# Six more key blocks with VectorE's exp, and a new written order, in an attention and gated-FFN kernel

## The chip, the cores and the metric

The kernel runs on one core of a Trainium2 chip. The metric is the device time of one launch in microseconds (us). The engines are TensorE (PE; its weight loads are shown apart as PEld), VectorE (DVE), ScalarE (ACT), GpSimd (POOL) and SyncE (SP), which starts most of the DMAs.

## The reference

```python
S, D, H, Dh, F = 2048, 512, 32, 16, 1792             # one batch, bfloat16
xn = layernorm(x)                                     # no gain, no bias
q, k, v = split(xn @ wqkv)                            # 32 heads of 16
p = softmax(einsum("qd,kd->qk", q, k) * Dh ** -0.5)   # for every head
attn = (p @ v).reshape(S, D) @ wo
gate, up = xn @ W_gate, xn @ W_up                     # 512 -> 1792
ffn = ((gate * (gate > 0)) * up) @ W_down
out = x + attn + ffn
```

The scores are 32 heads x 2048 x 2048, 134 million numbers, and each goes through an exp.

## The kernel before

**Tiling.** The 2048 queries are cut into four chunks of 512 (`c4`), the 32 heads into four groups of eight (`gg`), and each group into two halves of four heads (`ee`). That gives 32 rows, numbered 0 to 31 in the order (c4, gg, ee). A row runs over 16 key blocks (`kt`) of 128 keys. One key block of one row is four heads x 128 keys x 512 queries of scores. The layernorm, the projections of q, k and v, the gated FFN ("glu") and the output rows are background work, which stands between the attention's matmuls.

**Two kinds of key block.** A key block is done in one of two ways.

- *ACT's way.* Two units, each with scores of two heads in two banks of PSUM, one ACT exp over 128 x 1024 (L1365, `ring<-ps`), and then, when both units are there, one "PV stream" (`pv_stream`, L1244): eight matmuls of 64 x 32 weights on 512 columns, which add p @ v, and the row sums, into a bank of PSUM. PSUM has two places for the scores of a unit (pool `sc`, two banks each), so the scores of unit u+2 wait for the exp of unit u.
- *VectorE's way.* `quad` (L1312) makes four score banks, one at a time, out of the pool `b` of four banks that the projections, the FFN, the output and the PV sums use as well. A DVE instruction (L1320, "d1") adds a bias to a bank's scores and writes them as 16-bit integers, whose bits read as bfloat16 are a rough exp. Two more versions of all four banks together are made by adding a constant to the integers (one for each of two shifts): each either by one DVE instruction over 2048 columns (L1339, "d2" and "d3") or by two instructions of POOL (L1335, "p3"). All three versions go through PV, so that their errors average out: three PV streams instead of one.

The table `QUAD_AT` has one line for each row and one character for each key block. A dot is ACT's way. A digit is VectorE's way, and its bits say which of the two added versions POOL makes: 0 none, 1 the first, 2 the second, 3 both. The kernel before has 153 digits.

**The PE's tiles.** Nearly all matmuls use a 64 x 32 part of the array: four side by side in one half of its rows make one operation ("half"), and an operation of the other half may run at the same time. Scores of a key block are 16 matmuls, one PV stream is 8.

**The order.** No scheduler runs in the kernel: all engines' queues are in one written order. `PLAN` is a packed list that says, for each of its `PLAN_OPS` steps, which operation comes next, and for each operation that opens a buffer, which place of its pool it gets. `Graph.run` (L324) unpacks it, appends each operation to its engine's queue, and makes an operation that takes over a place wait for the ones that used it before:

```python
o = ops[at] if at < n else self.blank(at)
for t in o.acq:
    if t.slot is not None:
        continue
    t.slot = next(places)
    c = t.pool.cur[t.slot]
    if c is not None:
        for u in c.w + c.r:
            if u.eng != o.eng or o.eng not in ("PE", "ACT"):
                o.deps[u] = True
```

Each engine runs its queue in order, and waits on semaphores for what it needs of the others. A p3 of POOL also waits for the last d2 or d3 that stands ahead of it in the order. The integers lie in four buffers (pool `raw`), their added versions in five (pool `pat`), and ACT's exps in a ring of 16.

All matmuls of scores, PV, background and output are issued by one helper, L250. The last row is normalised at the end by DVE, PE and ACT (L1151 to L1168).

Of the kernel before, what the change touches and what calls it, by code (L numbers as in the profile page):

```python
# [16 lines left out]
S = 2048  # L17
D = 512
H = 32
DH = 16  # L20
F = 1792
# [25 lines left out]
NQ = 2  # L47
# [30 lines left out]
    "2...3..3..2..3..",  # L78
# [6 lines left out]
    "2...3..3..0..3..",  # L85
    "3...3..3..2..3..",
# [5 lines left out]
    "2...3..3..2..3..",  # L92
    "2...3..3..0..3..",
    "2...3..3..2..3..",
    "2...3..3..0..3..",
    "2...3..3..2..3..",
    "2...3..3..0..3..",
    "2...3..3..2..3..",
# [23 lines left out]
PLAN_OPS = 8248  # L122
PLAN = (
    "c-m!K1z;3M7v67n?{Wzd96~7)9Euky#fn1{v}hoK;8KbdcXx*Z#UWUc1S{?yij?ARg%p<nA>8f!Z)SJzHvEN<&E4+Ilka`+dvmFxr2dbKFK%6lf2^OxpPcvTGN*FSxG*2!#(Uzg@iI@fAXj{^<+x8@"
    "%6)Si-}BZZIh1?Wi;8boZof|$L0|XHm3{A9SJrLzy}8dF<9#T;*NnG~=Zyz+<6X!r<1XE12mQnqv4Rfy92EJAaiv>UfZpcj3mo26tqZQ$U$U%#_ciYGN&bQHBUf~J#l2=5&xoHaJB&+R@m)eUmxgY6"
    "1Mf<TVy*7=RX$=o=v_jrEyKoj@vvM?guuAZe1Kaql;**5!dTnG<bKeNI7+LmDA0wmjtHuEL0$U9ZE&$8Qryc8bEQY-YT!n=#1=+S<f4Xo@?W{UVg>|8pbR&RMXi6VU8KqKRjx=k#ie36ubayl(KlZZ"
    "Hkp@Zm}T5xJ)_w0XF*%xKB#iV=avr+x@m*ulCD_6H(%v;1K@*@uf*hc-3Kr$F6MW|ECM5~#yipxX1ho6K#?I4w=!QwxG%ZBoN;c4Gq+cx`6k)JEI2SPpBQc_9_EqpWxi+|cG5G(8XkzOFxxIx2)WG;"
    "v#>-|tRzVEh^;*em;WkE095*CSm<HqH|`M|cr09qT?N{VqVkBF%{%E!F2OyVSrjJo#C@^#5)-#ki(ELx!R42&{H1*&2Hxz52r$buahFFFHO%CC#9Q)JX4)?UB?Bn-@h~$EIv~rA8_Cs;WrYXK$Nit2"
    "M!^`XNhfIu!$pr-LS8yEID~)F1h<%6rs(#5!hPxRm9Y^lkGYG%5gr*R0~OLCGBU+!z=V64=^WYo$tfJMfyPTKzOG}v;bF$wOvcRc*~FY;Bv>(tiF*u~8(XJvKX15AfN<jhZuJo_&2ULV6kSIO6u07Z"
    "n^5&Yev|jYSj=N$RJvkR9J6dQw^K}4WnknQ2KJbTo4lwq%O)-%r<f?UuuDHk&%DjiSK&Se(yeb+R>Tduswg~lX?yeb(aF4Nkg+hqF8uHqwZ!ZoHmb)Pd?OPS5BUuDmX8s2!)cF~_zloVDiYqnivk~q"  # L130
    "nY1CwOy{3m@(zy-tptie8y<@zOv?m=nS1CyhNEu=B`7eOk-4-{f*<_M5>EDG7OrJlj3<qH<B}A0Uq6ShIT>w0_7VdV7WXDQb<H4KFK}%NhI8+iw?X?D-P<nA;$d8|bq!xzx2@%?Juea2d0J6Ycihz4"
    "iKpttb}qMXVl_42%G{@Q45=jhvlSWL=1(da;oV)g$rSi7X|g-_={ghMqMLJ*p}1~7rOW*c)nvS?_#*193-N&Jm2bY<vBgpM1wl8Rg-!aJs>hOTHhssvVvX}uy4D`TRBeJ=Dnik}C}X4+x2a?83x)z8"
    "P7M7D-$pVbhF-Mp(9NeUoO!Rm(9_&TEIgIe=U=4H*8F8n=~jp=p$ePY^|cgh5n-d%d3{m#82#JSWxiUqOr$1lsdSSV4fZs9w5f$mrt#t2l1_2~v;V<-Ua~WEtC}S<>(DK_7H`2Y3_dto2=#_e`(*Vt"
# [121 lines left out]
class Graph:  # L255
# [1162 lines left out]
```

## Time and profile before

| | |
|---|---|
| time, median of 3 runs (lowest to highest) | 685.26 us (685.21 to 687.11) |
| span of the profiled execution, first to last instruction | 684.2 us |
| busy, PE / DVE / ACT / POOL | 675.6 / 598.5 / 666.8 / 499.8 us |
| exps on ACT | 718 |
| d1 on DVE, d2 and d3 on DVE, p3 on POOL | 612, 83, 446 |
| matmuls on PE | 22262 |

The profile is of one execution; its own time is its span and about a microsecond around it. Matmuls are pipelined and their ends are modelled, so a PE that is busy is not a PE at its peak. A group's busy time is the union of its instructions; the mean ns of one is longer than union over count where instructions overlap. Lines (L1365) are those of the kernel before.

### The profile page before, as it was taken

The numbers are of one execution on the slowest core, as the hardware profiler recorded it, in microseconds if no ns is written. First come the engines' busy times: TensorE is split into PE (matmuls) and PEld (weight loads), VectorE is DVE, ScalarE is ACT, GpSimd is POOL, SyncE is SP. The second block draws the span as 40 slices with busy tenths as digits, with TensorE's granted clock in tenths as the row PEclk, the third lists the DMA queues.
The fourth block names the chain that finished last, engine by engine and source line by source line (L and its number), as shares of the span: only waits on it lengthen the run. The fifth ranks groups of instructions, "written<-read, shape, count | busy, mean of one in ns | idle before, by whom it ended". The sixth has DMA issues, their size and how long they took to land.

```text
span 684.2 us, 45020 instructions
## 1 busy us (share of the span) xinstructions
PE 675.6 (99%) x22262; PEld 345.9 (51%) x19654; DVE 598.5 (87%) x1012; ACT 666.8 (97%) x730; POOL 499.8 (73%) x507
## 2 busy tenths in 40 slices
PE   8999999999999999999999999999999999999998
PEld 4455454545555554554444455554554455555543
DVE  9958899999989787999999788889998887988875
ACT  6999999999999999999999999999999999999994
POOL 3323768678688778887587886888878868787792
PEclk9999999999999999999999999999999999999999
DMA  7430220113122021212101022120202012131011
GB/s 216 57 75 12 58 77 27 33 55 91 56 65 66 5 77 34 69 41 63 35 23 31 10 78 63 38 69 5 56 27 61 25 53 62 44 86 42 22 36 54
DMA packets 55940, 35.86 MB, mean 52 GB/s; under 512 B 19336, under 2 KB 51784, under 8 KB 55752
## 3 DMA queue, kind: packets, MB, share of 16 engines
q1 hardware_dynamic: 55464, 32.71, 17.4%
q8 instruction: 164, 2.69, 1.6%
q10 hardware_dynamic: 288, 0.26, 0.1%
q14 instruction: 24, 0.20, 0.1%
HBM read 26.35 MB, written 2.35 MB: 42 GB/s over the span
## 4 chain that ended last, share of the span: by engine, by line
PE 75%; ACT 18%; DVE 5%; issue 1%; DMA 0%; POOL 0%; ACTq 0%
PE ps L250 75%; ACT ring L1365 18%; DVE stats L726 1%; DVE qd L1320 1%; DVE xn_sb L739 1%; DVE v_aug L876 0%; DMA x_sb<-in_A_x_dram 0%; DVE qT L952 0%; DVE mv L727 0%; ACT xn_sb L1164 0%; DVE qd L1339 0%; DVE xnT L780 0%; POOL rstd L721 0%; DVE xnT L1075 0%; DVE kT L869 0%
## 5 line engine op out<-in xcount | busy, mean ns | idle before, releaser
L1365 ACT ACTIVATE ring<-ps 128x1024 bf16<-128x1024 f32 x718 | 660.4, 1141 | 2.9 <-PE ps L250 2.5
L1335 POOL TENSOR_TENSOR qd<-qd,ints 128x512 int32<-128x512 int32 x446 | 450.5, 1041 | 143.8 <-DVE qd L1339 73.2
L250 PE MATMUL ps<-qT,kT 64*32 64x512 bf16 x8192 | 448.7, 374 | 1.3 <-DVE qd L1320 0.4
L1320 DVE TENSOR_SCALAR qd<-ps 128x512 int16<-128x512 f32 x612 | 396.7, 685 | 51.9 <-PE ps L250 49.0
L250 PE MATMUL ps<-qd,v_aug 64*32 64x512 bf16 x3672 | 263.0, 375 | 1.1 <-issue 0.9
L250 PE MATMUL ps<-ring,v_aug 64*32 64x512 bf16 x2872 | 236.5, 374 | 0.1
L1300 PEld LDWEIGHTS <-kT 64*32 64x32 bf16 x7584 | 151.1, 92 | 126.6 <-issue 32.6
L1272 PEld LDWEIGHTS <-v_aug 64*32 64x32 bf16 x4544 | 108.7, 91 | 75.6 <-issue 20.4
L250 PE MATMUL ps<-xnT,wgs 64*32 64x512 bf16 x1792 | 137.6, 374 | 0.0
L250 PE MATMUL ps<-xnT,wus 64*32 64x512 bf16 x1792 | 136.4, 374 | 0.0
L250 PE MATMUL ps<-Wd,hT 64*32 64x512 bf16 x768 | 59.0, 375 | 0.0
L810 PEld LDWEIGHTS <-wgs 64*32 64x32 bf16 x1792 | 43.1, 91 | 31.5 <-issue 7.4
L810 PEld LDWEIGHTS <-wus 64*32 64x32 bf16 x1792 | 43.2, 91 | 29.8 <-issue 7.6
L1339 DVE TENSOR_SCALAR qd<-qd 128x2048 int16<-128x2048 int16 x83 | 56.1, 690 | 2.3 <-PE ps L250 2.2
L810 PEld LDWEIGHTS <-hT 64*32 64x32 bf16 x1792 | 40.2, 92 | 28.2 <-issue 4.2
L250 PE MATMUL ps<-Wv,hT 64*32 64x512 bf16 x512 | 45.7, 375 | 0.0
L250 PE MATMUL ps<-Wk,hT 64*32 64x512 bf16 x512 | 42.8, 375 | 0.4 <-DVE qd L1320 0.3
L1020 DVE SCALAR_TENSOR_TENSOR hT<-ps,up_sb 128x512 bf16<-128x512 f32 x56 | 38.4, 685 | 4.6 <-PE ps L250 4.2
L1016 DVE COPY up_sb<-ps 128x512 f32<-128x512 f32 x56 | 38.4, 685 | 3.1 <-PE ps L250 2.5
L250 PE MATMUL ps<-Wo_p,x_sb 64*32 64x512 bf16 x480 | 40.2, 374 | 0.6 <-issue 0.5
L250 PE MATMUL ps<-xnT,Wq 64*32 64x512 bf16 x480 | 36.2, 375 | 0.0
L250 PE MATMUL ps<-xnT,Wk 64*32 64x512 bf16 x480 | 35.0, 374 | 0.3 <-DVE xnT L780 0.3
(70 smaller groups left out, 263.8 us busy)
## 6 DMA issues: line engine op xcount, KB each, us to landing
rb<-rec_scr SPq DMA_DIRECT2D x31, 256.0 KB
wus<-in_B_W_up_dram SPq DMA_DIRECT2D x38, 128.0 KB, 2.8
wgs<-in_B_W_gate_dram SPq DMA_DIRECT2D x38, 128.0 KB, 3.3
xr_sb<-in_A_x_dram SPq DMA_DIRECT2D x16, 128.0 KB, 2.6
qT<-qf SPq DMA_DIRECT2D x120, 16.0 KB, 2.6
out_dram<-xn_sb SPq DMA_DIRECT2D x14, 128.0 KB, 2.0
x_sb<-in_A_x_dram SPq DMA_DIRECT2D x8, 128.0 KB, 2.8
x_sb<-oT SPq DMA_DIRECT2D x60, 16.0 KB, 2.5
```

The lines of the kernel that those rows point to most:

```text
L250: return e.add_instruction(mybir.InstMatmult(name=e.bass.get_next_instruction_name(), engine=mybir.EngineType.PE, ins=[e.lower_ap(x), e.lo ...
L726: G.op("DVE", 580, lambda e, m=m: e.bn_stats(stats[:, m, :], xs(m)), reads=[t_xm[m]], writes=[t_st], prio=pr, order=last_xn if m == 4 else ())
L739: G.op("DVE", 320, lambda e, m=m, t=t_n: e.tensor_scalar(xn_sb[:, t.slot, :], xs(m), mv[:, m, 0:1], rstd[:, m:m + 1], op0=ALU.subtract, op ...
L810: e.ldweights(w()[rows, 32 * j:32 * j + 32], tile_position=(rows.start, 32 * j))
L1016: G.op("DVE", 603, lambda e: e.tensor_copy(up_sb[:, tup.slot, :], bank_of(tu)), reads=[tu], writes=[tup], prio=-590)
L1020: G.op("DVE", 603, lambda e: e.scalar_tensor_tensor(out=hT[:, th.slot, :], in0=bank_of(tg), scalar=0.0, in1=up_sb[:, tup.slot, :], op0=ALU ...
L1272: e.ldweights(vs(j), tile_position=(64 * half, 32 * j))
L1300: e.ldweights(ks(m), tile_position=(64 * half, 32 * m))
L1320: G.op("DVE", 601, lambda e, j=j, tx=tx: e.tensor_scalar(qd[:, tq.slot, 512 * j:512 * j + 512], ps[:, BANK[tx.slot], :], IBIAS[3], 0.0, op ...
L1335: G.op("POOL", POOL_NS / POOL_PIECES + 60, lambda e, x=x, n=n, c=slice(i * m, i * m + m): e.tensor_tensor(x().bitcast(I32)[:, c], raw().bi ...
L1339: G.op("DVE", 600, lambda e, n=n, x=x: e.tensor_scalar(x(), raw(), float(SHIFTS[n + 1]), None, op0=ALU.add), reads=[ti, tq], writes=[t], p ...
L1365: exp_ops[u] = G.op("ACT", 904, lambda e, tr=tr, k0=k0: e.activation(ring[:, tr.slot, :, :], ps[:, 4 * k0:4 * k0 + 2, :], ACTF.Exp, scale= ...
```

## The change

The table gets six more digits, all of them 2, in rows 10, 17, 18, 25, 26 and 30, each time at key block 2. In these key blocks ACT's two exps go, and four d1 and one d2 on DVE, two p3 on POOL and two more PV streams on PE come in. The diff shows some rows as moved, because equal lines follow each other.

```diff
@@ QUAD_AT, rows 10, 17, 18, 25, 26 and 30, and lines between them
-    "2...3..3..2..3..",
+    "2.2.3..3..2..3..",
...
-    "2...3..3..0..3..",
-    "3...3..3..2..3..",
+    "2.2.3..3..0..3..",
+    "3.2.3..3..2..3..",
...
+    "2.2.3..3..0..3..",
+    "2.2.3..3..2..3..",
...
-    "2...3..3..2..3..",
-    "2...3..3..0..3..",
-    "2...3..3..2..3..",
+    "2.2.3..3..2..3..",
     "2..3..3.0..0....",
...
-PLAN_OPS = 8248
+PLAN_OPS = 8302
 PLAN = (
-    "c-m!K1z;3M7v67n?{Wzd96~7)9Euky#fn1{v}hoK;8KbdcXx*Z#UWUc1S{?yij?ARg%p<n...
+    ...
```

`PLAN` is replaced as a whole. Its 54 steps more are nine for each of the six key blocks: four d1, one d2, two p3 and four operations of PV, less the two exps. Counted in the two written orders, the queues hold:

| queue | before | after |
|---|---|---|
| ACT, exps | 718 | 706 |
| DVE, d1 and d2 or d3 | 612 and 83 | 636 and 89 |
| POOL, p3 | 446 | 458 |
| PE, operations of PV (four matmuls each) | 1636 | 1660 |
| SP, DMAs | 429 | 429 |

The same work of the background stands in both. The first 71 operations of PE, the first 64 of DVE, 15 of POOL and 21 of SP stand alike; behind them the order and the places of the buffers differ.

More of the change, by code (lines that the diff above doesn't have):

```diff
@@ new lines @@
+    "c-mcD2Ow4L8$ZuE_g>d7vZB4T&=4&tiYD5qq^+gBm0fAmPJ^_g5=G-nQizh$Rw=0zDl2jCIsf;4&pG$%{|Wb=^S;mf%-=K4^-<Kn|8e-66JOyU;ye7+`U85|n)<-M5H@i9J^YWq%>6@<qtw@06`^mcNH|8lU))0O"
+    "38$$~<r=T!5E1nKQQX3DAe_$qvw{5P0R3duH~%F>iAS@*3L@Yg6pKl+0`ufLi~pgkz`sGOSo}q{;vF0($VnD(EPjI)U`i}cieo`Ilw1NrofS@?1TKM42k}^PUt}L$C;JF-z^hm+I!DfAdBPm#oFlt=A{;1zFv<%{"
+    "gu~PTzZ3}L?fk)*Ch&sd<H%)v0Wf{M6~AWjnH<&_@GFVv!X|zLkqWOM>;q8@c}u9PWM=u}I9{DZZNRVQ_*?iF*T}zkv+;8A+9QXtAb1(a@eJ|DV73YKqI~2KUU3vr8_yoE7mh6AgiBa@at7W&tVER03g-ex%*paz"
@@ new lines @@
+    "K$a8r^5!8bQZdEy$`m|+oI?(6WO_k|{1T3LKS2=QgE>J8d@?y-5JnIXZB?p_A-cWV%>@nqb0|-XrTKgOE%dGA<x%qT5S!6NB(xo^RniR-Az1l<Q356SwQwBQNGdUGS>8=~{qjL3s7@4_*oVl4Sz_^-93Ldu^Uyn`"
+    "a0pAdp$IEVP<aG;$Ett^`!OdTh|LF>b;K$;gGOtKd@M(!S40FQAJ<CErji2DLzQ>|`Hi*_W|ib%;c%o8ifkgzBiIQM<>kWf@JT!k79<Uv7=(n55=79#1bGdqaSC0-+NT8oCRV5UfTe_BM3<FBF03H(iYOWck!Zp2"
+    "<Q<PCM6VRDVjTXwFxcGqCq@Zc!63w-xxX@g8Bd0n7V8)h|10B9<&8pY3RwFhXbEDd&{O1D0Aj%jH~}1x>N)-xOcLoH#1m<vbxNgL!6Y02Q6DFSCn1B~l0>@_V^U-E7o=BGG%*|RUpy@(G8KA7^KM1#gbl_Cprgu4"
@@ new lines @@
+    "_#)3Be~G08ZSz@!01!b=^qaUR@hsqD5tD6@5Gwd6LZ5I#2@)gIaiYZd4oeZ*g4+lbczxqNyvcEx(n8D<Wl(?QoRVhMUV*fs1OagbpQBXasmkmWTPNpuOcC8m3{fHpvIZr%4{{805>bR09Gr?#QF&xF_DRep%ksB~"
+    "&56xenm-ojL>eo-R?Z6Ei-V7&#T3o4EW`5Ilt(v_X_lyr76l_aIU!0}VoV%1y!Q|!BTz|;dKAgw<b`k7%4ps_#GHkwQGC282^|t(*tIa~P%4k$y^7{B1bZ>bqX-;@tfl0`kQkJs`D8$ljn^>2SzgIJUJ*E@gp4di"
+    "kpMQJN`T0p6|{&NoT@P54Xk9iT1~Zi|0$n1AqLSJ!3$V|kSt&7aN>0mO)Q^0ct|FZ%PAOjxg??(rH*$_C=}GLB@`{{RNrWqm|*!7!v9cbcAjBXN+87ysT_EW6w)})CneN(eCB02p}1hhqL3BJ4?d@onuiZs;CFCB"
@@ new lines @@
+    "QP-&ARmFhF{XdH43jsc-vy^y=M>7GB#1e~BRUDisDu^tr7*`jotg86rOFgbpeWu1${uK!I2%q#oz+avO2-*`j@WlAY0kLip(Tx(z6HcfiRoD1Rs!B(IY%B#{R;|Nl5;0qX=mkRk!z)OzH>)nn#2OmI2}UcH6YD}w"
+    "kVd6!k$bY7<BKmA_&kgpl_M#PM>ig8lpy2>jOY}o1XO~`_gGLN2uq3CL?tZ`3ltxV1X=ldm7@jVk^LbEg@KB^XN82wXC@^rmOOkKBO;3RHzrxBE0jnq$72A9K|p|s&=smMf|_E4;);_;eheF!E0*PR9}XXqk1(?e"
+    "hDT7oj3K7M$|0adax^AI6BR1?oX=-Kytzt`6Y__^j1qX`icqXn*W-NcPm|R`4a&zSzKMwA<jcn`;Z4D)@{iCKp!CL2N>y&<`0|`r2WFq8#j=sumdA98)YO<fDY_}K@&XmM5U>>zjZlrMeS+}ESBgAL(Mn=Ann>0_"
@@ new lines @@
+    "6Dtyw#^`|c#i@)X7Cjs#*oo8zeA~dP8)J@BLoKN!gi?p}eqzah4-wJ|5AA&IE|#(?pBEJ?_@r2H2+58W#3OA1$zY_?Qv)@nf-bgE-^~4LLY$A+5+{^Eyx#amf|MmfS10s-0x*jIga(QLpMZcu1<$FS17|0pxFdxZ"
+    "CxQj}=7ffeQ}-bvnhR~2P#j|4<-03Eeh><6evwMGLOaT-`VXp+9=Lx;6T&&X5aJ?UpTu{C#uW)59L#&C==tJuPUtFGPIPXe3**%7oml*;08N|^2vEzj(|EAKiRJ>avgB=#&#RZJ!BL>g+gPYDIRRM&8923@h}rm$"
+    "hN|dR+fxmJjeEpKkj-(dIF9)DGDm^B&ZpF)AywWG+7&gJlQ9X`DDQBp>RDZpidm5p#Rb(J(XK*~#HkG{aKYE%oN%0QjL>8^s)tlHjj9n5YXxB(B5n~aB8)DCVu)2om4NK5I+LgxZ%!C@h@CK~3vV9F_>zN9^knM9"
@@ new lines @@
+    "HYzlDm5I``AQlF~+=XO({v_3as<9n8mBf7g_>a08H|d-pbfX%C`y;2=Mi%A%$;v8$#EArP5C8!;xJErTX$VONFG847m^e{1OQ{yIJj4qXH0cibx{$BZ$?%EgU-MH6Qc+VvfzJ2G6rbpL=ogw&K4OU#NTy(g(jLDO"
+    "2PtCJ&BL$I`~cr>3gr$(iGWS<=qOA;IMK-|Rf|g|Y-00Gk!4~S()=(-C`Tx9L__iv$)w`khF7aFtsv>0r6|>qhZ4b-mk^f*w2+(y0Bq#v0+JG6=4tWERLO%RQsDxxUBO!jK@RvUf)>T9o`ptSaKaR@@$^RM{lsIa"
+    "28NF&W#g%j7!_*Y;I-etaOznu--@b>UNuDVRSqRqYGR|xw_mi_;;~|DO|m%8f;fCsP2j{Vp`>_$K`A7B;*vskC9SHu^%Q(kj0wIK=QuGhuxbbqk~S|TsYdv;$+vyNWRe#^7-8}yBP-4{RD{HwMX7yPKzdQp!VMAs"
@@ new lines @@
+    "`GJ{|5{ofVPi!&eYF$2m@&UtwYQQaI3;_WJ+l%)^;1DLG6sZryfvwmfi1S>*+r);NRnM2nMO3izKBZt(=t@$(c(SVZ6U-&LtO!S(*qTymLkh0lsCna5U@nNqsnH*VxrtyQaaN{AbHP>l5ape@QOhLaCYh2o>bDyY"
+    "S6Fpv$P*N0YlPNZqZ)x+`zzyAm7X|ESKCA!rE`s+$Ox1hKZ9wU*8eZni|rL9jz?JzSXDJ9J_Hd*XT0U1(NKas_7If?+&{A=lB(E7qk2{>V}#TBXBEWJ3CakZkTQU8E1=P%38D1m8flDG4+$E#<(#@-7X)Qh&eurW"
+    "LZ8fuO?#tyL>%9PdWcQ^3qNA5z|!iXg%i4T5c^fJzHam^N+=r|JxF6I>YqnaD)uN9E^>_?W3im*`%0i1)nU{>pxS5@@{fav2})@B$Q%^-d?Adc#PPS#hVhe9!GV>4`)x9x#Hyr~B<rfD=HwpVZt`<LGQuRoKhjGI"
@@ new lines @@
+    "^FmG>7LyS&?gN3(q_~7-X%Vl5zE9v)7!@j2V@{#mMwU_lEl%LbxRWoN#qlHX6qK~O#pFk?AV8cjH3uPmE1_{o$7g+UVh+MMljI4ZFd^9yM}d%qDAhm+#M*_QdEzv}!!d}%B@iDkQv8!T5wisVr1-Zi%W(XYEFj|q"
+    "q3WiD{G;k+sYWfMs#oDu)uVvU!V@J*JycUaf)dW<Xf=-fQ_NETIvUq#_Sk3yNc}VUSEqN56CP!W_dyL+ypM^Ks>VY?b$pNlhEznHy0KEHBcNFIL=1$%g2*UKHNs@R^8P0(RQ-x-+`@CiQflxKBar3`H<q95@slF%"
+    "pCyeRFE`eMy3+%(v*A?u(<u4{wW#}TRlg$676mgmYPSBb3sONwV~lKEVo{AzxiRbiHZf|FjdKX6dT1y<&QVP)S<zyR(xU*ptT-`MH=dLs{QKW08OR!HfI%TmcLj!J7&hBRBGLTIu$uMIrck26m_QM<{sbC$xv@m4"
@@ new lines @@
+    "p+x^=&)Z7g(qLMFu1OW>2aSH?1$xQ~x*1KsY%7t`&%hAfZwkKwTGF6jMT0gvhT-yhJ+y;tbSB8aly-;(Xzh^UKwn2x&~NkwbpTGW(+~D(T5j}P`+j#;_M{v1kZGkg1!yy9<O+GiM`*44({S~a4u!4sOSP0mGH6}c"
+    "R*QY4XK4H*XW(C5%{r|gAlH^%>IabvO>PZLeYm74T@Tki7dVW(=Ji)zb#=^Dw_2k!V@=}Rpz_>kotr^vOJafj21f(F^?=uDeXh|Flgt7krw>Goi(%c9Lbk36t@pfHI!3><7A%`CVNZ;uX<2XR9ogq;Eqe`^unqpk"
+    "S=T}~{;iu=O>=enUq-?eT93&aU|bf<I1ZB<!qNNQ2j<p?ZTjI0whxkz*!Hya%$8o(7y+-M<%u6!eX6>?vPDVG?G+`9quLgFcy|a^_)G>xTs-UTeNsLVPMloxpmVg32D)};hyL8HfqtbYPCc7#qhRm!*H{7GKdv<m"
@@ new lines @@
+    "ZdN(duv&MgLXi`v<J+Y+7~t-*F?3ze&}qwHi|q8|ICtqLNO(DYRE{)2LT`l4?d;CRPL4ABwp6|}JtyL%|GY!6-S^Fb9J^i3VZttEneC%9Tv$Ny(miV>KF14No=+ZSn_1GkY~pav$uo1}g}y<D{0A}Mm$mJnSxI35"
+    "Sof*8U@f&>+HLQmg_S{jW?3$)eE_`;Dvc`EL6mQ|rMF>dUHfm9QA=;jfE}*bzBHt`OK*sc*=pmovv+LFe~|OX=1rbow*5gPx0!SIr6!LmFIznJeEYDWkT<XByM0^mlC2(R2Y;t53jqE0MJ=DrJ$!xn@m{?@o(al2"
+    "z3mC~2rF+}8Td#kp{<^EHFySQbQD}lO>uXkw>D$ou!sL(N!sFVX;AQIb?i^03OlIM>$96)sMY5`t$y1;3(h1z+!|W1usd{Yzs=FvxnZNge{fhv=7q`_Lui#cbi<aSG0D)n!znN}W36S$ka%1%CH8W~e`hE9fWpvm"
@@ new lines @@
+    "yp!+qY<nv@z^+C1jA^}xLD7#Li;dlrVN5x6WbX_OvM?X=;l6|Mk2gJy!@Sbp&44z?*0B*@bj$4joGu6Do111zz0Owk`y8>_>C;UIN%d>X{Qh#^l^uUKeQg3SZCg4=e<)vf4-|I><=>d+(T+`quAydaG9kS7PQ~_P"
+    "Fe7|mhQsq$t7jg(m2S}0@(o-}3C`+k0aD{Kx^C(z{ioKE0ndK5iy63fiw%4?sIAhRbcQpoJG&g<>#(F64O-R`at##qG1D~d=N!pt({b+_I{PI!!Qyj&w?8<XJ3iOy%uq1NTa)?Pggx()k`Xp3i?+RPy2t0y)t#@U"
+    "2B259BRlqYN&n+ZYqkAGCHnjx3Fq!?e`)lrSKfmVrWxF5c5=ktfL{kL!3`a{%4z)a0jtK*_Hg~nokh}I81c-F&UA*doLuYvaZ65q>+A;KjS^{-l(~<m#sn0<n0wf$-16(VXZsdbfB9l>8{O9cmLGg3lUKgleHN<P"
@@ new lines @@
+    "DkbnXd`^>!4nHj+b7Rzk#lJiChwNU`TQZ}$+pFzz#=@a_UtYC+Revz-@f^5#kmI%$(UPw{J#tIjyCz?CPqY{ZnYQ~|Ek7=$y$dbitfbhYp>Kxo#R>6aM@z;_V4UnsY`X!T>@f{R#p<}Jn~Mf&SDg3BoZrC&%A4)|"
+    "Bk7$t>3oktVB?wVSYH@h|J)wFWsLBh_;`Hyle`<*E8A4-#=z<bM;Y5ZwX3XMHSBfHZVM2ens0Nru*W{XHu}=LW5FX(me}!aFJ~s_!=$DIj@;9s6;ZLK2%8?-J3iI8G3we(*uP-LY`ANv$gvpVdu`;xM@OS0;qZ+3"
+    "F5FB-U~>FV$nU<hG{&QcAJcTzIyV#NdBN;DIxzI7!3Np7@HJZ-!j&<O<MSrA)hQb~%xwOF#aHP~E*qtR$(E<~gRg1Ttb-|D?ICl&({m^@xp8o91v7Ni6-nyBed`Z>Z<o}m)!0kz>9=s;N1tvF4<CHpwH1U;`zx!r"
@@ L221 @@
+    "l^r;BBQjEwsx@%R{~x15F?|")
 class Pool:
```

161 lines of the change are left out of this document (66 added, 95 removed).

## The prediction, made before the change was run

> **What bounds the kernel now.** I read the page's busy shares first, then its groups, then the busy time of each engine in stretches of 20 us, and last the waits. The page alone misleads:
>
> ```profile
> span 684.2 us, 45020 instructions
> PE 675.6 (99%) x22262; PEld 345.9 (51%) x19654; DVE 598.5 (87%) x1012; ACT 666.8 (97%) x730; POOL 499.8 (73%) x507
> PE 75%; ACT 18%; DVE 5%; issue 1%; DMA 0%; POOL 0%; ACTq 0%
> ```
>
> TensorE (PE) is busy 99% and carries 75% of the chain, so it looks like the bound, with ScalarE (ACT) at 97% beside it. The groups of the instructions that the change touches:
>
> ```profile
> L1365 ACT ACTIVATE ring<-ps 128x1024 bf16<-128x1024 f32 x718 | 660.4, 1141 | 2.9 <-PE ps L250 2.5
> L1335 POOL TENSOR_TENSOR qd<-qd,ints 128x512 int32<-128x512 int32 x446 | 450.5, 1041 | 143.8 <-DVE qd L1339 73.2
> L1320 DVE TENSOR_SCALAR qd<-ps 128x512 int16<-128x512 f32 x612 | 396.7, 685 | 51.9 <-PE ps L250 49.0
> L250 PE MATMUL ps<-qd,v_aug 64*32 64x512 bf16 x3672 | 263.0, 375 | 1.1 <-issue 0.9
> L250 PE MATMUL ps<-ring,v_aug 64*32 64x512 bf16 x2872 | 236.5, 374 | 0.1
> L1300 PEld LDWEIGHTS <-kT 64*32 64x32 bf16 x7584 | 151.1, 92 | 126.6 <-issue 32.6
> L1339 DVE TENSOR_SCALAR qd<-qd 128x2048 int16<-128x2048 int16 x83 | 56.1, 690 | 2.3 <-PE ps L250 2.2
> ```
>
> The first row decides it. 718 exps take 660.4 us as a union, 0.920 us each (one lasts 1141 ns, but the next begins before it ends), and ACT was idle ahead of them for only 2.9 us in all. Is ACT then following PE, or PE following ACT? The stretches answer; columns after the length are PE, PEld, DVE, ACT and POOL busy us, each with its count of instructions, then granted clock, DMA share and GB/s:
>
> ```profile
> 40.00:60.00 20.00, 20.00 (x696) 11.29 (x680) 12.37 (x20) 20.00 (x23) 1.62 (x3) 1.00 0.18 50
> 320.00:340.00 20.00, 20.00 (x652) 9.21 (x564) 19.37 (x33) 20.00 (x23) 11.82 (x12) 1.00 0.19 50
> 227.00:247.00 20.00, 20.00 (x720) 11.00 (x630) 15.61 (x26) 20.00 (x23) 14.13 (x15) 1.00 0.09 26
> 368.00:389.00 21.00, 20.83 (x680) 9.02 (x561) 17.11 (x28) 20.90 (x24) 17.14 (x18) 1.00 0.07 21
> 389.00:410.00 21.00, 20.10 (x716) 11.70 (x624) 16.41 (x27) 20.09 (x23) 18.34 (x19) 1.00 0.22 63
> 532.00:552.00 20.00, 19.89 (x644) 8.75 (x568) 15.92 (x27) 20.00 (x23) 14.40 (x15) 1.00 0.08 19
> 552.00:572.00 20.00, 20.00 (x716) 11.50 (x628) 15.45 (x25) 20.00 (x24) 16.55 (x17) 1.00 0.15 45
> 633.00:654.00 21.00, 21.00 (x744) 11.88 (x643) 16.47 (x29) 21.00 (x24) 16.73 (x18) 1.00 0.12 37
> sum 123.00, PE 121.83 PEld 63.85 DVE 96.97 ACT 121.99 POOL 97.29; mean PE 20.30 PEld 10.64 DVE 16.16 ACT 20.33 POOL 16.21
> ```
>
> In 20 us PE does 644 matmuls in one stretch and 720 in another, both with 23 exps and both "busy" for 20 us. The exps keep one pace; PE's matmuls stretch to fill it. So ACT bounds, and PE has hidden room: its densest stretch, 720 in 20 us, is 27.8 ns a matmul, where the whole run has 675.6 us / 22262 = 30.3 ns. At 27.8 ns all 22262 would take 619 us, some 56 us less than PE's busy time. The granted clock is 1.00 throughout, so that is no slow clock. But the room is thin in places: 389 to 410 has both the most matmuls and 0.91 us of idle ACT.
>
> **What goes: exps.** Six key blocks, in rows 10, 17, 18, 25, 26 and 30 of the table (counted from 0), change from ACT to VectorE (DVE). Each had two exps, so 12 of 718 go: 12 x 0.920 = **11.0 us** of the engine that bounds. The last six rows above are those rows' stretches, placed by counting exps from the first at 10.9 us. [...]
>
> **What is added.** For each of the six, by the table's mark 2: four d1 and one d2 on DVE, two pieces of p3 on POOL, and three PV streams of 8 matmuls instead of one; the 16 score matmuls only change their place.
> - PE: 6 x 16 = 96 matmuls; at 27.8 to 30.3 ns that is 2.7 to 2.9 us, spread over 22358. Where PE has room it costs nothing.
> - DVE: 24 d1 at 396.7/612 = 0.648 us and 6 d2 at 56.1/83 = 0.676 us: 15.6 + 4.1 = 19.6 us. DVE's idle time is 684.2 - 598.5 = 85.7 us in all, so there is cover overall. In the six stretches alone there is not: 123.0 - 97.0 = 26.0 us idle, less the 11.0 us by which they shorten, is 15.0 for 19.6.
> - POOL: 12 p3 at 450.5/446 = 1.01 us, 12.1 us beside 184 us idle: nothing.
> - No DMA is added; SyncE's queue keeps its 429 transfers, in a new sequence.
>
> **What is moved.** The new written order answers the shortage. I counted, in both orders, the matmuls and the DVE instructions of 512 columns or more between the first score of one row of the table and the first of the next. The six rows hold 153 such DVE instructions before and 162 after: of 30 new ones only 9 stay, 21 push other work (GLU evictions, other quads) into neighbouring rows. PE's matmuls in rows 10, 17, 18, 25, 26, 30 go from 708, 640, 716, 648, 712, 704 to 684, 596, 736, 632, 708, 652.
>
> **Where PE becomes the bound.** A score pair can be made only two exps ahead, so PE must fit into each row's exps. A changed row has 20 exps, 18.4 us. At the densest pace seen, 27.8 ns:
> - row 18: 736 matmuls, 20.5 us, over by 2.1;
> - row 26: 708, 19.7 us, over by 1.3;
> - row 10: 684, 19.0 us, over by 0.6;
> - rows 17, 25 and 30 fit, as do all rows with 22 exps (20.2 us): the fullest, row 11, has 724 and needs 20.1.
>
> That gives back **4.0 us** of the 11.0. In the order of before no row is over. Bounds: nothing, if the excess is absorbed by the row next to it, and 2.9 us more, if every added matmul also costs its 30.3 ns. I take 4.0, since each row's excess is reckoned from the densest row of the windows. [...]
>
> **Weight loads.** The new order keeps a loaded weight less often: 5435 groups of four loads instead of 4884, some 2200 LDWEIGHTS more. The cheapest end is nothing; the dearest, at 151.1/7584 = 20 ns of union time each, would be 44 us. The row from 40 to 60 decides: 680 loads for 696 matmuls, nearly one each, and still 23 exps with ACT never idle. I take nothing.
>
> **Fuller VectorE rows.** Rows with 32 or more such DVE instructions rise from one (row 7, 33) to six (rows 7, 9, 29 with 33; 15, 16, 23 with 32). From 320 to 340 DVE ran 33 instructions in 20 us beside 23 exps, so this fits, but without slack. An instruction late there holds one of the four banks that scores for DVE, projections and PV share; behind it in PE's queue stands the next score pair, and behind that the exp.
>
> ```profile
> ACT ring L1365 <- PE ps L250: 2.5, 6, 0.9
> DVE qd L1320 <- PE ps L250: 49.0, 112, 1.8
> POOL qd L1335 <- DVE qd L1339: 73.2, 37, 20.1
> ```
>
> The first row prices it: ACT waited for PE six times, 0.42 us each, 0.9 at most. One such wait in each of the five newly full rows is **2.1 us**; bounds nothing and 4.5 us. The second row says that DVE today more often waits for PE than PE for DVE. POOL's waits for d2 are kept off the end by its idle time.
>
> **Opening and end.** The first 71 PE operations and the first 64 of DVE stand where they did; from there, about the sixth exp, the order is new, but the table's rows 0 to 9 keep their marks and their matmuls change by at most 24 a row. The end is still PE and DVE normalising the last row. I take 0 for both.
>
> ```profile
> 649.12 25.12 ACT L1365 ACTIVATE ring<-ps 128x1024 bf16<-128x1024 f32 x27
> 680.25 0.60 ACT L1164 ACTIVATE xn_sb<-ps 128x512 bf16<-128x512 f32 x1 [6.00 <-PE ps L250]
> ```
>
> About 10 us follow the last exp, ended by ACT's wait of 6.0 us for PE; the order has 66 PE operations behind the last scores instead of 60, and six operations of four matmuls are 24 x 27.8 ns = 0.7 us at most, if none of them fits into that wait.
>
> **The sum.** -11.0 + 4.0 + 2.1 = -4.9 us, so the profiled span would go from 684.2 to 679.3. The three timed runs have a median of 685.26, 1.1 us over that span; the same distance gives **680.4 us**.
>
> **Rivals.**
> - *The whole 11.0 us arrives* (674.3): the excess of rows 18 and 26 is smoothed out and DVE never holds a bank too long. For it: ACT idled only 2.9 us with DVE at 87%. Against it: the 0.91 us that ACT lost from 389 to 410, where matmuls were densest. Chance 0.14.
> - *Forecast*: ACT still paces, PE paces three rows; 676.5 to 683.2. Chance 0.60.
> - *A wash*: the two give-backs reach their upper bounds, 4.0 + 2.9 + 4.5 = 11.4 against 11.0, 685.7. Chance 0.11.
> - *Slower, PE is the true bound*, as 99% busy and 75% of the chain say. Then the exps that go are worth nothing, since each pair of scores leaves PE no sooner, and 96 matmuls at 30.3 ns add 2.9 us: 688.2. It decides from the point where PE has no room in most rows, not in three. For it: in the new order the matmuls per exp rise in most rows. Against it: 644 and 720 matmuls beside the same 23 exps. Chance 0.10.
> - *Slower, DVE paces*: all 19.6 us of its new work lie on the path, 19.6 - 11.0 = +8.6, 693.9. It needs DVE without idle time in nearly all rows; it has 85.7 us. Chance 0.05.
> - *No change in the work*: excluded, the order has 706 exps.
>
> A measurement of this kernel can tell about 0.3%, 2.1 us, so "same" is 683.2 to 687.3. Faster is 0.14 + 0.60 = 0.74, same 0.11, slower 0.10 + 0.05 = 0.15. The range for 8 in 10 runs from 675.0, inside the full gain, to 687.0, past the wash: left out are about 0.07 below and 0.13 above.
>
> **What would show it.** The exp group with 706 and about 650 us of union, 0.92 each; a step up to 0.93 or more tells what was given back. In the stretches of rows 18 and 26 ACT's waits for PE should rise, by some 2 and 1 us, with over 700 matmuls in 20 us; in rows 17, 25 and 30 the 20 exps should take about 18.4 us. ACT's waits for PE over the run should grow from 2.5 us to between 5 and 9. POOL's group has 458, d1 636, DVE about 618 us. The forecast is wrong if the exps keep 0.92 us in row 18 (PE had more room than 27.8 ns), or if they slow in rows that were not changed and hold no more than 690 matmuls (then DVE or the new buffer places do it), or if the span does not fall although 12 exps went.

## The result, and the profile after

The changed kernel takes 703.06 us (median of four runs, 702.00 to 704.26); the kernel before, run beside it, 685.83 us (685.21 to 687.11). The ratio is **1.025, 95% interval 1.0229 to 1.0271: slower by 17 us**, where 4.9 us faster was forecast. The profiled execution took 704.26 us, 1.8 us more than its span. All ratios below are of this kind, against runs of the kernel before on the same chip. On the chips of the experiments the kernel before took 687 to 688 us, so ratios and not times are compared, and 1% is 6.9 us. Runs that were disturbed are left out of the ratios.

From the page of the changed kernel: the span, the busy times, the chain by engine, and the groups that answer to those of the prediction.

```profile
span 702.5 us, 47322 instructions
PE 685.6 (98%) x22355; PEld 389.1 (55%) x21858; DVE 622.3 (89%) x1042; ACT 666.4 (95%) x718; POOL 512.6 (73%) x519
PE 80%; DVE 12%; POOL 4%; DMA 2%; issue 1%; ACT 1%; ACTq 0%; DVEq 0%; POOLq 0%
L1373 ACT ACTIVATE ring<-ps 128x1024 bf16<-128x1024 f32 x706 | 660.1, 1040 | 20.6 <-PE ps L258 17.5
L1343 POOL TENSOR_TENSOR qd<-qd,ints 128x512 int32<-128x512 int32 x458 | 462.3, 1040 | 137.5 <-DVE qd L1347 86.9
L1328 DVE TENSOR_SCALAR qd<-ps 128x512 int16<-128x512 f32 x636 | 413.6, 684 | 48.4 <-PE ps L258 41.5
L1308 PEld LDWEIGHTS <-kT 64*32 64x32 bf16 x7980 | 166.6, 92 | 112.1 <-issue 25.7
L1347 DVE TENSOR_SCALAR qd<-qd 128x2048 int16<-128x2048 int16 x89 | 64.8, 737 | 0.3 <-PE ps L258 0.2
```

Twelve exps are gone, yet the exp group's union is 660.1 us as before (660.4). Its row says why: ScalarE (ACT) was idle ahead of exps for 20.6 us instead of 2.9, for PE, and it is 1% of the chain, not 18%. The waits give the number and the longest of these:

```profile
ACT ring L1373 <- PE ps L258: 17.5, 34, 1.3
DVE qd L1328 <- PE ps L258: 41.5, 91, 1.7
POOL qd L1343 <- DVE qd L1347: 86.9, 46, 22.8
```

34 waits instead of 6. The stretches of the six changed rows, in the order 10, 17, 18, 25, 26, 30, placed by counting exps (columns as in the prediction):

```profile
235.00:255.00 20.00, 20.00 (x704) 13.10 (x692) 17.14 (x28) 19.48 (x21) 14.08 (x14) 1.00 0.02 5
378.00:399.00 21.00, 19.95 (x604) 10.42 (x556) 18.02 (x30) 19.08 (x22) 15.98 (x17) 1.00 0.11 31
399.00:421.00 22.00, 22.00 (x768) 12.59 (x748) 18.46 (x30) 19.66 (x21) 19.99 (x20) 1.00 0.14 38
546.00:566.00 20.00, 19.76 (x660) 10.98 (x632) 17.51 (x30) 18.78 (x21) 14.17 (x15) 1.00 0.08 20
566.00:586.00 20.00, 19.86 (x700) 11.48 (x664) 16.81 (x27) 18.43 (x21) 16.64 (x18) 1.00 0.15 44
651.00:670.00 19.00, 19.00 (x672) 11.69 (x644) 16.43 (x29) 19.00 (x22) 15.98 (x17) 1.00 0.10 28
```

The clock is 1.00 throughout. From first exp to first exp, the rows took (us, worked out from the two traces):

```
row                10     17     18     25     26     30  | six   | 0 to 2 | other 23
before          20.05  20.59  21.25  20.16  20.19  20.21  | 122.5 |  75.9  |
after           19.43  20.83  21.40  19.86  20.42  18.47  | 120.4 |  80.6  |
difference      -0.6   +0.2   +0.2   -0.3   +0.2   -1.7   |  -2.0 |  +4.7  |  +14.7
```

Only row 30 took the 18.4 us of its exps. But most of the loss is not in the changed rows: rows 0 to 2 lose 4.7 us, and the other unchanged rows 0.64 us each; of these rows 9 (22.73 instead of 20.74), 31, 29 and 28 lose most (row 31 is taken to the end of the last exp). A single row differs between executions: in e11, which is the changed kernel again, rows 17 and 19 took 22.71 and 23.41 us instead of 20.83 and 21.42, while rows 0 to 2 lost 4.4 and row 30 took 18.72.

### The profile page after: what moved, and what is told of

Its sections match the earlier page's. It is cut to its first block, busy times and chain, and to the rows that moved or that the text cites. A ratio compares the mean times of both kernels' runs of the same rounds, so it can differ in the third digit from the quotient of the medians.

```text
span 702.5 us, 47322 instructions
## 1 busy us (share of the span) xinstructions
PE 685.6 (98%) x22355; PEld 389.1 (55%) x21858; DVE 622.3 (89%) x1042; ACT 666.4 (95%) x718; POOL 512.6 (73%) x519
## 4 chain that ended last, share of the span: by engine, by line
PE 80%; DVE 12%; POOL 4%; DMA 2%; issue 1%; ACT 1%; ACTq 0%; DVEq 0%; POOLq 0%
PE ps L258 79%; DVE qd L1328 6%; POOL qd L1343 4%; DVE stats L734 1%; DVE qd L1347 1%; DVE xn_sb L747 1%; ACT ring L1373 1%; DMA rb<-rec_scr 1%; PE ps L916 1%; DMA rsum<-o_sb 1%; DVE up_sb L1024 1%; DVE hT L1028 1%; DVE v_aug L884 0%; DMA rec_scr<-rrec 0%; DVE o_sb L1206 0%
## 5 line engine op out<-in xcount | busy, mean ns | idle before, releaser
L1373 ACT ACTIVATE ring<-ps 128x1024 bf16<-128x1024 f32 x706 | 660.1, 1040 | 20.6 <-PE ps L258 17.5
L1343 POOL TENSOR_TENSOR qd<-qd,ints 128x512 int32<-128x512 int32 x458 | 462.3, 1040 | 137.5 <-DVE qd L1347 86.9
L258 PE MATMUL ps<-qT,kT 64*32 64x512 bf16 x8192 | 478.9, 375 | 3.7 <-DVE qd L1328 1.2
L1328 DVE TENSOR_SCALAR qd<-ps 128x512 int16<-128x512 f32 x636 | 413.6, 684 | 48.4 <-PE ps L258 41.5
L258 PE MATMUL ps<-qd,v_aug 64*32 64x512 bf16 x3816 | 316.0, 375 | 0.4
L258 PE MATMUL ps<-ring,v_aug 64*32 64x512 bf16 x2824 | 247.3, 375 | 1.0 <-DVE v_aug L884 0.9
L1308 PEld LDWEIGHTS <-kT 64*32 64x32 bf16 x7980 | 166.6, 92 | 112.1 <-issue 25.7
L1280 PEld LDWEIGHTS <-v_aug 64*32 64x32 bf16 x6352 | 153.9, 92 | 92.5 <-issue 20.2
L258 PE MATMUL ps<-Wd,hT 64*32 64x512 bf16 x768 | 65.1, 375 | 1.1 <-issue 0.5
L1347 DVE TENSOR_SCALAR qd<-qd 128x2048 int16<-128x2048 int16 x89 | 64.8, 737 | 0.3 <-PE ps L258 0.2
L258 PE MATMUL ps<-Wk,hT 64*32 64x512 bf16 x512 | 46.4, 375 | 0.2 <-DVE qd L1328 0.2
```

The costliest lines, as they stand in the source:

```text
L258: return e.add_instruction(mybir.InstMatmult(name=e.bass.get_next_instruction_name(), engine=mybir.EngineType.PE, ins=[e.lower_ap(x), e.lo ...
L1280: e.ldweights(vs(j), tile_position=(64 * half, 32 * j))
L1308: e.ldweights(ks(m), tile_position=(64 * half, 32 * m))
L1328: G.op("DVE", 601, lambda e, j=j, tx=tx: e.tensor_scalar(qd[:, tq.slot, 512 * j:512 * j + 512], ps[:, BANK[tx.slot], :], IBIAS[3], 0.0, op ...
L1343: G.op("POOL", POOL_NS / POOL_PIECES + 60, lambda e, x=x, n=n, c=slice(i * m, i * m + m): e.tensor_tensor(x().bitcast(I32)[:, c], raw().bi ...
L1347: G.op("DVE", 600, lambda e, n=n, x=x: e.tensor_scalar(x(), raw(), float(SHIFTS[n + 1]), None, op0=ALU.add), reads=[ti, tq], writes=[t], p ...
```

## The experiments

Three theories stood at the start. The first, called 'order' below: the new written order makes PE wait in its queue for banks that DVE has not freed. The second, 'weights': the new order loads weights more often, and PE has no room for it. The third, 'marks': DVE cannot carry the six new key blocks.

**e1, every weight loaded anew, in the kernel before.**

```
-            elif held[o.half] == o.wkey:
+            elif False:
```

> The kernel before, with every operation's weights loaded anew: 5536 groups of four loads instead of 4884, that is 652 more, where the change adds 551. Order, marks and places are those of before. Theory 'order' (the new written order makes PE wait in its queue for banks that DVE has not freed): loads are hidden, 685 to 688 us. Rival 'weights' (the loads are the 23 us between the forecast of 680 and the 703 measured): 23 x 652/551 = 27 us more, about 712 us. Rival 'marks' (DVE's six more key blocks themselves): no change, 685 to 687.

Ratio 1.0185 (1.0157 to 1.0212): 652 more groups of four loads cost 12.7 us, 19.5 ns each, with the same matmuls and the same order. That is neither nothing nor the 27 us of the rival 'weights'.

**e2, the old order up to row 10, the new one behind it.** (`PLAN` is rebuilt: operations of rows 0 to 9 as before, then as after.)

> The change's kernel, with the old order and places up to the first scores of row 10, and the new order behind them; 159 marks. Rows 0 to 9 have the same marks in both kernels, and the traces reach row 10 at 228.1 us before and 235.6 us after. Theory 'order', with a loss that arises where the order is new: 7.5 us come back, 695 to 697 us. Rival 'marks': rows 0 to 9 hold no new mark, so nothing comes back, 702 to 704. Rival 'weights': part of the added loads goes, 696 to 700.

Ratio 1.033 (1.0307 to 1.0353). Rows 0 to 8 ran as in the kernel before, the rows behind as in the changed one; but the splice jammed row 9 (30.2 us), and the time lies outside all three forecasts. It only shows that rows 0 to 8 owe their loss to their own order.

**e3 and e4, the marks alone, the order alone.** e3 has the 159 marks in the old order; e4 the new order with the six blocks put back.

```
e3:  - QUAD_AT, PLAN of before     + QUAD_AT of after,  PLAN: old order, six blocks respread by hand
e4:  - QUAD_AT, PLAN of after      + QUAD_AT of before, PLAN: new order, twelve units put back by hand
```

> The 159 marks in the old order: the six key blocks' new operations are put in at the place that the new order gives them relative to the scores around, and in rows 9 to 11, 16 to 19, 24 to 27 and 29 to 31 the score pairs are spread evenly over PE's other work; everything else stays in the old order and keeps its old places where they are free. 5002 groups of loads. Theory 'order': most of the forecast gain comes, 677 to 684 us. Rival 'marks': DVE can't carry the six, 695 us or more. Rival 'weights': 118 more groups than before cost 5 us of the 11 that go, about 680.

> The new order and its places with the 153 old marks: the six key blocks go back to ACT, their exps and scores put in at the same places, score pairs spread evenly in the six rows. 5418 groups of loads. Theory 'order': it loses what the change loses and has 12 exps more, 700 to 714 us. Rival 'marks': without the six, DVE has room again, 684 to 690 us. Rival 'weights': as the theory, 705 to 714.

Ratios 1.1953 and 1.0883: misses. My hand-made places jammed rows: seven rows of e3 and two of e4 took 14 to 22 us longer, so nothing on the marks follows. One thing can be read: row 0, with no jam near it, took 34.06 us in e4, which has the old marks (30.05 before, 33.56 after). The order, not the marks, costs what the opening loses.

**e5, load groups left out of the changed kernel**, which brings its loads to the count of before (the list has 581 groups; the page counts 2268 loads less, 567 groups).

```
+            elif o.idx in SKIP and held[o.half] is not None:
+                o.load, o.wsrc = False, ()
```

> The change's kernel, order, marks and places as they are, but 581 groups of weight loads are left out: those of operations whose weights the kernel before still held (they then multiply whatever weights stand there, so the output is not the reference's). 4868 groups of loads stay, about what before has (4884). Reloading 652 groups in the old order cost 12.8 us, 19.6 ns a group. Theory 'weights are half of it': 581 x 19.6 ns = 11.4 us come back, 691 to 693 us. Rival 'weights are all of it': 680 to 684. Rival 'waits on banks, not loads': 700 or more.

Ratio 1.0236 (1.0199 to 1.0273): nothing measurable comes back, where the cost of a group in e1 let 11.4 us be expected.

**e6, the old order in rows 0 to 2 of the changed kernel**, spliced at a place with no jam.

> The change's kernel with the old order and places in rows 0 to 2 and the new ones behind; what the new order had done earlier keeps its old place. The traces reach row 3 at 86.8 us before and 92.0 after, 3.5 us of it in row 0. Theory 'the opening's new order loses 5 us by itself': 697 to 699 us. Rival 'the loss moves elsewhere': 701 to 704.

Ratio 1.0206 (1.0169 to 1.0242), 3.0 us less than the changed kernel; the intervals allow anything from about 0 to 6 us. In the trace rows 0 to 2 recover 4.5 us and the six changed rows 1.1, while the other rows lose 3.3 (rows 9, 11 to 13 and 28 most).

**e7 and e8, DVE's first step cut**, in the changed kernel and the one before.

```
-  lambda e, j=j, tx=tx: ... qd[:, tq.slot, 512 * j:512 * j + 512], ps[:, BANK[tx.slot], :]
+  lambda e, j=j, tx=tx, w=512 if u < 90 else 256: ... 512 * j:512 * j + w], ps[:, BANK[tx.slot], 0:w]
```

> The change's kernel, but from the 90th exp on each d1 of VectorE does 256 of its 512 columns (the rest of the integers is stale, so the output is not the reference's). Each d1 gets some 0.25 us shorter, about 125 us less DVE time in all. Theory 'PE waits for banks that DVE holds': nearly all that is not weight loads and opening comes back, 686 to 692 us. Rival 'DVE is no part': 700 or more.

> The kernel before with the same shortened d1. Theory 'ACT paces, DVE is covered': 680 to 686 us, a few us of the 14 by which the exps lag their best pace. Rival 'DVE holds PE up in the old order too': 675 or less.

Ratios 1.0215 (1.0165 to 1.0266) and 0.9971 (0.9956 to 0.9985). The kernel before gained 0.3%; the changed one 0.35%, which lies within its interval. DVE's first step, though it took 126 us less (622.3 to 495.7 us of DVE's busy time), holds neither kernel by more than that.

**e9 and e10, exps cut**, in the changed kernel and in the one before; **e11 and e12**, which were to have shorter matmuls of PV.

```
e9, e10:   - ring[:, tr.slot, :, :], ps[:, 4 * k0:4 * k0 + 2, :]
           + ring[:, tr.slot, :, 0:w], ps[:, 4 * k0:4 * k0 + 2, 0:w]        (w = 384 from u = 90)
e11, e12:  no line differs from the changed kernel, and from the kernel before
```

> The changed kernel, in which every exp of ScalarE from the 90th unit on works on 768 of its 1024 columns (384 of each bank); the columns left out are never written, so the output is not the reference's. Nothing else changes. About 616 exps then take some 0.69 to 0.75 us instead of 0.904 to 0.920, 95 to 130 us of ScalarE in all. [...] Theory B (ScalarE still paces and loses time to many small late scores, which its own speed lets it catch up): 650 to 675 us.

> The kernel before with the same shortened exps (768 of 1024 columns from the 90th unit on; the output is not the reference's). [...] Theory B expects the same sort of gain as in the changed kernel, to 640 to 665 us. If it does not move at all (683 to 687), TensorE sets the kernel before as well and the prediction's bound was wrong from the start.

> The changed kernel, in which the matmuls of scores with values from the 90th unit on have 384 instead of 512 columns, except the first and last of each sum (the output is not the reference's). Some 5,700 matmuls lose a quarter of their 27.8 ns: about 40 us less work for TensorE, with the same number of instructions, loads, waits and places. Theory A (TensorE's queue sets it): the time falls by 15 to 30 us, to 672 to 688, where ScalarE's 706 exps at 0.904 us begin to pace. Theory B (ScalarE paces with small late scores of other causes): 697 to 703.

> The kernel before with the same shortened matmuls of scores with values (the output is not the reference's). Theory A: its 718 exps at 0.904 us and the 36 us ahead of the first exp are 685 us, which is its time, so it hardly moves: 681 to 687. Theory B: it moves as the changed kernel does, by 0 to 5 us. If it falls by more than 10 us, TensorE held the kernel before too.

e11 and e12 do not test what is expected of them: their kernels are the changed kernel and the kernel before without any edit, and PV's matmuls in the trace of e11 have all their 512 columns:

```profile
L258 PE MATMUL ps<-qd,v_aug 64*32 64x512 bf16 x3816 | 318.3, 375 | 0.6 <-issue 0.2
L258 PE MATMUL ps<-ring,v_aug 64*32 64x512 bf16 x2824 | 247.9, 375 | 0.9 <-DVE v_aug L884 0.9
```

So whether the length of PE's matmuls sets its queue was not tested. What e11 and e12 give is a repeat: the change has ratio 1.0272 (1.0224 to 1.032) on another chip, and the kernel before against itself 0.9999 (0.9987 to 1.0012).

Ratios with exps cut: changed 1.0278 (1.0257 to 1.0298), before 0.9933 (0.9912 to 0.9953). In e9 ACT's busy time fell from 666.4 to 582.0 us, and the changed kernel is no faster than its repeat e11 on the same chip: ACT does not pace it, and theory B's 650 to 675 us did not come. The kernel before gained only 0.7%, so PE stood close behind ACT there too. Its 683.18 us miss theory B's 640 to 665, and lie at the edge of what the expectation called no move at all, by which TensorE sets the kernel before as well. (The 36 us that e12's expectation puts ahead of the first exp do not lie there: it starts at 10.9 us.)

**e13 to e16, all other engines cut at once.** No single relief had shown anything in the changed kernel, so the question became whether PE's new queue needs the time by itself.

```
e13, e14:  exp as in e9; d1 as in e7; d2, d3:  - x(), raw()     + x()[:, 0:w], raw()[:, 0:w]   (1024 of 2048)
           p3:  - c=slice(i * m, i * m + m)    + c=slice(i * m, i * m + m // 2)                (256 of 512)
           all from u = 90 on
e15:       e13 with the SKIP of e5             e16: the changed kernel with the cut of p3 alone
```

> The changed kernel, in which from the 90th unit on every other engine's share of attention is cut: exps on 768 of 1024 columns, VectorE's first step of a key block on 256 of 512 and its shifts on 1024 of 2048, GpSimd's shifts on 256 of 512 (columns left out are not written; the output is not the reference's). TensorE's queue, its loads and all waits stay. Theory W (the new order makes TensorE wait for ScalarE, VectorE and GpSimd at many places, so that no relief of one engine shows): 670 to 686 us, within 6 us of the kernel before with the same cuts. Theory P (TensorE's queue by itself needs the time: how halves follow each other, loads behind waiting operations, instruction packets): 694 to 704, and 12 us or more over the kernel before with the same cuts.

> The kernel before with the same cuts on ScalarE, VectorE and GpSimd (the output is not the reference's): what TensorE's old queue needs by itself. With shorter exps alone it took 683 us. Theory W: 670 to 683. Theory P: the same here, since it only says that the new queue needs more: 670 to 683.

> The changed kernel with all these cuts and without 581 of its groups of weight loads (those of the earlier run; the output is not the reference's). Theory P, if the extra loads are what the new queue costs: 8 us or more below the cuts alone. If it is how halves and waits follow each other, or theory W: within 4 us of the cuts alone.

> The changed kernel with only GpSimd's shifts cut, to 256 of 512 columns from the 90th unit on (the output is not the reference's): the trace shows GpSimd's chains on the path at 213 to 225, 383 to 392 and 528 to 535 us. Theory W with GpSimd as the main waiter: 690 us or less. Theory P, or W without a main one: 698 to 704.

| | median us | ratio (95%) |
|---|---|---|
| e14, before, others cut | 676.64 | 0.9829 (0.9813 to 0.9845) |
| e13, changed, others cut | 698.26 | 1.0138 (1.0111 to 1.0165) |
| e15, e13 without 567 load groups | 688.84 | 1.0016 (0.9994 to 1.0037) |
| e16, changed, p3 cut alone | 704.14 | 1.0244 (1.0204 to 1.0285) |

This is the main evidence. With ACT, VectorE and GpSimd relieved together the two orders still differ by 3.09% of the time of the kernel before, 21 us, and the changed kernel is still slower than the whole kernel before was: **PE's new queue needs more time even where the other engines have room.** The relief has limits. It starts at the 90th exp, which comes at 94.7 us in e14 and at 99.3 in e13, so 4.6 of the 21 us lie where nothing is relieved. And the DMAs are not relieved; PE's waits of over 150 ns for them add up to none in e14 and 1.4 us in e13. Busy rows of e13 and e14, and their waits of ACT for PE:

```profile
PE 675.8 (98%) x22358; PEld 378.5 (55%) x21858; DVE 464.7 (67%) x1042; ACT 580.4 (84%) x718; POOL 330.5 (48%) x519
ACT ring L1373 <- PE ps L258: 76.7, 214, 1.7
```

```profile
PE 664.5 (98%) x22262; PEld 352.3 (52%) x19654; DVE 449.6 (67%) x1012; ACT 593.3 (88%) x730; POOL 322.8 (48%) x507
ACT ring L1365 <- PE ps L250: 36.9, 118, 1.2
```

ACT, VectorE and GpSimd are at 48 to 88%, ACT waits for PE in both, and PE is "busy" 98% in both. Now the loads show: e15 gains 1.22%, 8.4 us, 15 ns a group, where e5 without the cuts gained nothing measurable.

e16 is a warning about the chain. In the changed kernel it has long pieces of GpSimd (start us, length us, what):

```profile
213.60 1.28 POOL oT L1240
214.88 0.78 POOL qd L1343
215.84 2.81 POOL qd L1343 x3
218.83 6.03 POOL qd L1343 x6
224.95 0.70 DVE qd L1328
383.23 9.02 POOL qd L1343 x9
```

Cutting all these shifts by half from the 90th exp on moved nothing measurable (1.0244 against 1.025).

**e17 and e18: the opening, and the price of a load.** e17 is e6 with the cuts of e13; e18 is e1 with them.

> The changed kernel with the old order in rows 0 to 2 (as in the earlier run, at the new buffer places behind the splice) and with the cuts on ScalarE, VectorE and GpSimd from the 90th unit on (the output is not the reference's). With the cuts alone the changed kernel took 698.3 us, the kernel before 676.6, and without 581 groups of loads 688.8. If the new order behind the opening is part of what TensorE's queue costs (row 0 took 3.5 us more), the time is 694 to 695; if it is lost again further on as without the cuts: 697 to 700.

> The kernel before with these cuts and with every operation's weights loaded anew (652 more groups of four loads; the output is not the reference's). At the 9.4 us that 581 groups were worth in the changed kernel with the cuts (16.2 ns a group) the 676.6 us become 687; if additional loads only cost time where ScalarE paces, as in the earlier run with reloads (12.8 us), it stays within 4 us of 676.6.

e17 has ratio 1.0056 (1.0032 to 1.0081; median 690.57 us): the new order of the opening costs 0.82%, 5.6 us (7.7 us by the medians; 694 or more was expected). In the traces e13 loses 4.9 us in rows 0 to 2 against e14, and e17 nothing. These rows lie ahead of the 90th exp, so nothing shows that PE needs this time by itself, and the waits below speak against it. Against e14 e17 still needs 2.27%, 15.6 us, more, and these lie behind the 90th exp. e18 has 1.0047 (1.0024 to 1.0071; median 690.61): 2.18% over e14, 15 us for 652 groups, 23 ns each. With the other engines relieved, loads cost time in both orders.

What the opening loses can be seen. From 24 to 46 us, in the kernel before and then in the changed one:

```profile
24.00:46.00 22.00, 21.77 (x724) 11.43 (x676) 15.94 (x30) 21.98 (x25) 7.73 (x13) 1.00 0.39 62
```

```profile
24.00:46.00 22.00, 19.21 (x608) 10.06 (x604) 17.50 (x30) 19.06 (x21) 7.36 (x10) 1.00 0.35 50
```

608 matmuls instead of 724, 21 exps instead of 25, at the same clock. PE's waits in that stretch of the changed kernel, and one of them in the timeline:

```profile
PE ps L258 <- DVE v_aug L884: 1.4, 3, 0.9
PE ps L258 <- DVE qf L861: 1.3, 1, 1.3
```

```profile
42.34 0.69 DVE L861 TENSOR_SCALAR qf<-ps 128x512 bf16<-128x512 f32 x1 [0.51 <-PE ps L258]
43.83 0.41 PE L258 MATMUL ps<-xnT,Wk 64*32 64x512 bf16 x4 [1.31 <-DVE qf L861]
```

In the new order PE reaches PV before DVE has cast the v that it needs, and a projection of k before DVE has emptied a bank of q. The kernel before has no such wait of PE in that stretch.

## Why the prediction was wrong, step by step

- **"PE has hidden room, some 56 us"**: the step that failed first. The room was read from the densest stretch, 27.8 ns a matmul. With the other engines cut, the old queue took 676.6 us (e14), 1.7% below the time of the kernel before: 12 us of room, as far as these cuts show it, not 56. Matmuls at their densest pace are not what PE's queue needs; loads belong to it as well (e15, e18), and so do waits like those of the opening. That ACT paces the kernel was right only to a small extent: the kernel before gains 0.7% by shorter exps alone (e10), 0.3% by a shorter d1 alone (e8) and 1.7% by all cuts together, not 8%. One reading behind the step was wrong too: the stretch from 389 to 410 us, with its 0.91 us of idle ACT, is not where matmuls are densest. It has 716 in 21 us, 34.1 a us; the stretches from 227 to 247 and from 633 to 654 have 36.0 and 35.4, with ACT busy throughout. PE's busy share does not tell the runs apart: it is 97 to 99% in all runs here but the jammed e3 and e4 (92 and 95%), whatever their time. The loads' share, 51% before and 55% in the changed kernel, points the right way, but e5 brought it back to 52% with no measurable gain.
- **"Weight loads: I take nothing"**: mis-sized. Measured: 12.7 us for 652 groups in the old order (e1), 15 us with the cuts (e18), 8.4 us for 567 in the new one with the cuts (e15 against e13); in the changed kernel as it is, nothing measurable (e5). The row from 40 to 60 us showed only that ACT was not late there, not that PE could do the same everywhere. The upper bound of 44 us was far too high.
- **"Opening: I take 0"**: wrong. Rows 0 to 2 lost 4.7 us with unchanged marks; the order alone does it (e4's row 0, and rows 0 to 2 in e6 and e17).
- **"-11.0 for the exps"**: the exps went, but ACT no longer set the time, so they were worth nothing (e9). The exp pace of 0.92 us rose to 660.1/706 = 0.935.
- **"4.0 us in rows 18, 26 and 10"**: PE did overrun them, but by more: 21.40, 20.42 and 19.43 us where 20.5, 19.7 and 19.0 were reckoned. Rows 17 and 25, which "fit", took 20.83 and 19.86 instead of 18.4. Only row 30 was right. The kernel before did not keep to the reckoning either: its rows 17 and 18 took 20.59 and 21.25 us where 22 exps should have taken 20.2.
- **"2.1 us of ACT's waits in rows with a full VectorE"**: the cause was another. ACT's waits rose by 15 us, not by 2.1, and a faster d1 changed next to nothing (e7). DVE's 622.3 us of busy time (618 expected) and the counts 706, 636, 458 came as said.
- **The rivals.** "PE is the true bound", chance 0.10, was right in kind for the changed kernel. Its price, 2.9 us for 96 matmuls, was wrong: it charged the matmuls and not their order. The condition it named, no room in most rows, fits e13 as a whole. Of the things that would make the forecast wrong, two came: the span did not fall although 12 exps went, and rows that were not changed and hold no more than 690 matmuls slowed (row 9, with 648, by 2.0 us); but the second was put down to DVE or the buffer places.

**How far the 21 us are accounted for** (e13 against e14): loads 8.4, the opening 5.6, of which its 30 fewer groups are 0.4 and counted already; the 96 added matmuls 2.7 at 27.8 ns, an estimate. That is 16.3, if the parts simply add up, which no run tested; **some 5 us stay open**, about the size of the intervals. Part of them may be DMAs in their new sequence: PE's waits for DMAs are 1.4 us in e13, 3.1 in e17 and none in e14. Not measured is also why, without the cuts, e5 gave back so little. One reading would be that in the changed kernel the waits between PE and the others lie so close that when one goes the next takes its place. That is argued, not shown: in e7 PE's waits for d1 fall from 3.7 to 1.8 us, and the waits of weight loads for which the profile shows no releaser ("PEld ... issue") rise from 67.5 to 71.3, but in e11, the same kernel again, they are 75.7. What the six marks alone cost is open too, since e3 jammed. No version that leaves nothing out was faster than the kernel before.

## What to carry to other kernels

An engine that hardly idles looks like the bound (here ACT, idle 2.9 us ahead of its exps), but this doesn't say how much room the next one has: its densest stretch flatters it, and cutting the work of all the others at once gives a better measure (here 1.7%, not 8%). When the queue of that next engine is rewritten, price the whole of its new sequence: loads that no longer find their weights, operations reached before their bank is free, and rows nobody meant to change. Where relief of one engine shows nothing, that doesn't clear it; relieve several together before ruling a cause out. And an experiment counts only when its trace shows the change that it was to make: e11 and e12 had none, and their times looked like an answer.

## What the runs showed of the hardware that was not expected

A group of four weight loads had no single price. The prediction took it as nothing; the runs gave four answers:

| | groups | us | ns a group |
|---|---|---|---|
| e1, kernel before | 652 more | 12.7 | 19.5 |
| e18 against e14, kernel before with the other engines cut | 652 more | 15 | 23 |
| e15 against e13, changed kernel with the other engines cut | 567 fewer | 8.4 | 15 |
| e5, changed kernel as it is | 567 fewer | nothing measurable | |

One load of kT lasts 92 ns in the traces of both kernels; in the kernel before the loads are busy for 345.9 us and the matmuls for 675.6, in a span of 684.2, so at least 337 us of the loads' time lie beside matmuls. No run separates what makes up the price of a load, and none tested how halves follow each other or the instruction packets, which e13's expectation names beside the loads. Why the price differs was not shown.
